# Gates and ups of a GEGLU block as pairs of 64-row half tiles

## The chip, the cores and the metric

The kernel runs on one core of a Trainium2 chip. The metric is the time of one execution on the device, in microseconds (us). A time is the median of several executions. Beside it stands one profiled execution of the same program, with its own time, its span (from the first instruction to the last) and a record of each instruction. PE is TensorE, DVE is VectorE, ACT is ScalarE, POOL is GpSimd and SP is SyncE, which here only starts DMA transfers. PEld stands for the weight loads of PE.

## The reference

One transformer layer on 2048 tokens of 448 features, in bfloat16. Attention and feed-forward block read the same normalised input and are added to the residual.

```python
xn = layernorm(x)                                     # x: [1, 2048, 448]
qkv = xn @ wqkv                                       # 16 heads of 28
scores = (q @ k^T) * 28**-0.5, kept where 0 <= i - j < 256
attn = (softmax(scores) @ v) @ wo
ffn = (gelu_tanh(xn @ w_gate) * (xn @ w_up)) @ w_down # 448 -> 1792 -> 448
out = x + attn + ffn
```

The gate and up products are the part that the change touches. Both contract over 448 features, which is three times 128 and a rest of 64. Each has 1792 output features, or 14 tiles of 128.

## The kernel before, in words

The 2048 tokens are worked through in four blocks of 512 (`qb` 0 to 3). The normalised input is held transposed in `xnT`, with features on the partitions. It has four chunks. Chunks 0 to 2 hold 128 features each. Chunk 3 holds the last 64 features twice, on the partitions 0 to 63 and again on 64 to 127.

**Order of the work.** Each block has an attention stage (`attention`) and then a gated stage (`gated`). In the attention stage PE computes scores (L612), ACT takes their exponentials (L618), and PE multiplies them with the values (`pv`, L572). Between the steps PE is fed with other work from generators in `Feed` objects. `share` and `drain` take from them by budgets written out by hand (`plan`, `PROJ`, `DOWN`, `UP1`). In block 0 this other work is the block's own q and k projections, some of its up products ("early" ups, `gen_up`, tile `ue`) and the projections of block 1. In blocks 1 and 2 it is the down projection of the block before (`gen_down`, tile `po`, L371 and L376) and the next block's projections. In block 3 it is a down projection and early ups. After the last gated stage the last down projection runs alone.

**Gates and ups.** An output tile needs three matmuls with 128 rows of features (`three`, which calls `mm3`, L228) and one with 64 rows (`half`, which calls `mm_half`, L234). The 64-row matmuls are issued in twos: one on the lower 64 rows of the PE array and one on the upper 64 rows. They share the array, and each writes its own PSUM bank. The weights of the last 64 features are therefore kept in `wgu3` and `wug3`, which hold gate and up rows on opposite halves of the partitions. Work goes in pairs of neighbouring output tiles, `f` and `f + 1`. `gated` collects the 64-row matmuls of two or three pairs into one stretch: the groups are (0, 2), (4, 8, 6), (10, 12) in blocks 0 and 3, and (0), (2, 4), (6, 8), (10, 12) in blocks 1 and 2. For the first pair of blocks 1 to 3 the 64-row matmuls are cut to 32 columns, the tile form that the `pv` matmuls behind them have. ACT applies the gelu (L460), and DVE multiplies with the up product (L467). An early up is copied from PSUM into `hT` by a DVE cast (L411), and is multiplied there later.

**PSUM banks.** There are eight banks. In the gated stage the gates use two tiles of two banks each (tag `s`). The ups, early ups, projections, `pv` and the down projection share two banks of tag `m` and one each of tags `d` and `o`. In the attention stage the scores take the four banks of `s`. In blocks 1 to 3 the early ups and projections then have the two `m` banks, which `pv` also uses for its two halves. There ACT copies one half (L556) and DVE adds the other to it (L557).

**Loads.** SP starts nearly all transfers in one order, and its transfers run in that order. Ahead of the first attention stage these are: x, the projection weights, `wu` with the up rows of `wug3` and `wgu3`, x of tokens 1024 to 1535, and a small piece of k weights (`w3k`). Behind them come four transposes of the normalised input of block 1 (L215), then x of the last tokens, gate weights, `wo` and `wd`.

A second path (`general_path`, entered when the plain softmax could overflow) isn't entered in the runs shown.

Of the kernel before, what the change touches and what calls it, by code (L numbers as in the profile page):

```python
# [16 lines left out]
P = 128  # L17
# [58 lines left out]
def kernel(  # L76
# [45 lines left out]
    def rows(w, c0, n):  # L122
        return w[c0 * P:(c0 + n) * P, :].rearrange("(c p) n -> p c n", p=P)

# [55 lines left out]
    xnT = const.tile([P, 4, S], bf16, name="xnT")  # L180
    qT = const.tile([P, 4, S], bf16, name="qT")
# [171 lines left out]
    UP1 = 1660  # L353
# [36 lines left out]
    def half(ps, f, gate, hi, ts, start, stop, m=P):  # L390

        w3 = wgu3 if gate != bool(hi) else wug3
        mm_half(ps, w3[:, f * P:(f + 1) * P], xnT[:, 3, ts], hi, start, stop, m)

    def three(ps, f, gate, ts, start, stop):
        w = wg if gate else wu
        mm3(ps, lambda c: w[:, c, f * P:(f + 1) * P], lambda c: xnT[:, c, ts], start, stop)

    def gen_up(qb, fs):

        ts = slice(qb * QB, (qb + 1) * QB)
        for f in fs:
            us = []
# [6 lines left out]
            for i in range(2):  # L410
                nc.vector.tensor_copy(out=hTs[qb][:, f + i, :], in_=us[i][:, :])  # L411
            yield -360

    def gated(qb, early, last_v, flush, hook):

        ts = slice(qb * QB, (qb + 1) * QB)
        hT = hTs[qb]
        turn = ["o" if down_tag[0] == "d" else "d", down_tag[0]] * 4

        def single(name, tag):  # L420
            return psum.tile([P, QB], f32, name=name, tag=tag, bufs=2 if tag == "m" else 1)[:, :]

        def begin(f, apart=False):
            last_tag[0] = turn[0] if f not in early else last_tag[0]
            pr = dict(f=f, us=[])
            if apart:
                pr["gs"] = [single("g0", tag) for tag in ("m", turn.pop(0))]
                return pr
            pr["gt"] = phase[0].pool.tile([P, 2, QB], f32, name="gt", tag="s")
            pr["gs"] = [pr["gt"][:, i, :] for i in range(2)]  # L430
            if f not in early:
                tags = ("m", turn.pop(0))
                if qb == 0 and f == 0:
                    tags = [ring[0][(ring[1] + i) % 3] for i in range(2)]
                    if "d" in tags:
                        turn.insert(0, "o")
                pr["us"] = [single("u0", tag) for tag in tags]
            return pr

        def dense(pr, start):  # L440
            f = pr["f"]
            gs = [(g, f + i, True) for i, g in enumerate(pr["gs"])]
            us = [(u, f + i, False) for i, u in enumerate(pr["us"])]
            for ps, fi, gate in (gs + us if f else us + gs):
                three(ps, fi, gate, ts, start, not start)

        def halves(pr, start, m):
            f = pr["f"]
            for i in range(2):
                if pr["us"]:  # L450
                    half(pr["gs"][i], f + i, True, 0, ts, start, not start, m)
                    half(pr["us"][i], f + i, False, 1, ts, start, not start, m)
                else:
                    half(pr["gs"][i], f + i, True, i, ts, start, not start, m)

        def end(pr):
            f = pr["f"]
            ge = work.tile([P, 2, QB], bf16, name="ge", bufs=2)
            if "gt" in pr:
                nc.scalar.activation(out=ge[:, :, :], in_=pr["gt"][:, :, :], func=ACT.Gelu_apprx_tanh)  # L460
            else:
                for i, g in enumerate(pr["gs"]):
                    nc.scalar.activation(out=ge[:, i, :], in_=g, func=ACT.Gelu_apprx_tanh)
            if not pr["us"]:
                nc.vector.tensor_tensor(out=hT[:, f:f + 2, :], in0=ge[:, :, :], in1=hT[:, f:f + 2, :], op=ALU.mult)
            for i, u in enumerate(pr["us"]):
                nc.vector.tensor_tensor(out=hT[:, f + i, :], in0=ge[:, i, :], in1=u, op=ALU.mult)  # L467
                flush()
            hook(f)

        for fs in ((0, 2), (4, 8, 6), (10, 12)) if qb in (0, 3) else ((0,), (2, 4), (6, 8), (10, 12)):
            prs = [begin(fs[0])]
            dense(prs[0], True)
            prs += [begin(f, len(fs) == 3 and f == fs[1]) for f in fs[1:]]
            for pr in prs:
                halves(pr, pr is not prs[0], 32 if qb and not fs[0] else P)
            if not fs[0]:
                last_v()
            end(prs[0])
            for pr in prs[1:]:  # L480
                dense(pr, False)
                end(pr)
# [49 lines left out]
    def attention(qb, feeds, aux, plan):  # L532
# [52 lines left out]
        if qb:  # L585
            feeds[0].run()
        steps = list(steps_of(qb))
        pvs = {4: 0, 6: 1, 9: 2} if qb else {4: 0, 7: 1, 10: 2}
        for i, (scores, ncol, edges) in enumerate(steps):
# [38 lines left out]
            if left == 1:  # L628
                drain(feeds)
            elif not qb:  # L630
                share(feeds + [Feed()], 1e12, 0)
            else:
                to = plan.get(i, 0)
                whole = sum(f.left for f in feeds) + STEP * left + PV * sum(j > i for j in pvs)
                ahead = STEP + PV * (i + 1 in pvs) + (360 if to > 1000 else 0)
                late = 400 if i == 0 else 0
                want = (whole - late) / (left + 0.2) + late - ahead - to
                if i in pvs:
                    had = feeds[0].left
                    share(feeds[:1], min(1100, want), 0)  # L640
                    want -= had - feeds[0].left
                share(feeds, want, to)
# [57 lines left out]
    transp(3, 1, nc.vector.tensor_copy, "d")  # L700
    pvs.append(alone("pv", "o"))
# [50 lines left out]

    for qb in range(NB):
# [11 lines left out]
        if qb == 0:  # L765
            new_hT(0)
            early = (2, 4, 8)
            feeds = [Feed((gen_qk(0, (1, 2, 3), [(t, pvs[t]) for t in (2, 3)]), 3 * QK1 + 360),
                          (gen_up(0, (2, 8)), 2 * UP1), (gen_proj(1), PROJ), (gen_up(0, (4,)), UP1))]
        else:  # L770
# [63 lines left out]
    with tc.If(n_ok < 1, preferred_fallthrough_block=True, label="general"):  # L834
        general_path(tc, locals_=dict(x_sb=x_sb, xnT=xnT, qT=qT, kT=kT, v_sb=v_sb, wg=wg, wu=wu, wgu3=wgu3, wd=wd, wo=wo,
                                      ident=ident, outv=outv))


def general_path(tc, locals_):
# [4 lines left out]
    with ExitStack() as st:  # L844
# [11 lines left out]
        for qb in range(NB):  # L856
            ts = slice(qb * QB, (qb + 1) * QB)
            for f in range(NF):
                fs = slice(f * P, (f + 1) * P)
                pg = ps.tile([P, QB], f32, name="pg", tag="pg")  # L860
                pu = ps.tile([P, QB], f32, name="pu", tag="pu")
                for i, (dst, w) in enumerate(((pg, L["wg"]), (pu, L["wu"]))):
                    for c in range(3):
                        nc.tensor.matmul(dst[:, :], lhsT=w[:, c, fs], rhs=xnT[:, c, ts], start=(c == 0), stop=False)
                    p0 = 64 * i
                    nc.tensor.matmul(dst[:, :], lhsT=L["wgu3"][p0:p0 + 64, fs], rhs=xnT[p0:p0 + 64, 3, ts], start=False, stop=True,
                                     tile_position=(p0, 0))
# [78 lines left out]
```

## Time and profile before

| | |
|---|---|
| median of 3 executions | 221.18 us (221.12 to 221.22) |
| the profiled execution's own time | 221.11 us |
| its span | 219.4 us |
| mean granted TensorE clock | 0.998 |
| PE busy | 213.0 us, 97% of the span, 2281 matmuls |
| DVE busy | 152.3 us, 69% |
| ACT busy | 133.3 us, 61% |
| POOL busy | 48.8 us, 22% |
| share of PE in the chain that ended last | 93% |

The profiled execution's own time is 1.7 us above its span. What the span says of a change can so be added to 221.11 us, which stands 0.07 us below the median. A matmul record is longer than the distance to the next one, because matmuls overlap at their ends. So the starts of matmuls tell more of PE's pace than their durations do.

### The profile page before, as it was taken

How to read it: one execution, taken by the hardware profiler on the slowest of the kernel's cores; microseconds unless marked ns; L12 is line 12 of the kernel's file. 1: busy time of each engine (PE TensorE's matmuls, PEld its weight loads, DVE VectorE, ACT ScalarE, POOL GpSimd, SP SyncE). 2: the span in 40 equal slices, each digit the busy share in tenths (PEclk: the TensorE clock that was granted, in tenths of full speed). 3: DMA queues.
4: the chain of work that ended last, by engine and by line, in shares of the span. 5: the costliest groups of instructions: out<-in, count | busy, mean ns of one | idle time of the engine just before them, and what ended most of it. 6: DMA issues, size and time to landing. Idle time of an engine off the chain costs nothing.

```text
span 219.4 us, 5439 instructions
## 1 busy us (share of the span) xinstructions
PE 213.0 (97%) x2281; PEld 95.6 (44%) x2281; DVE 152.3 (69%) x345; ACT 133.3 (61%) x131; POOL 48.8 (22%) x83
## 2 busy tenths in 40 slices
PE   6999999999999999999999999999999999999993
PEld 2433333444444454444444445444344445444562
DVE  5987896799666883679565795386356799479521
ACT  3588788662878875432878888233486777565000
POOL 5767987320000120022000022021000022022001
PEclk9999999999999999999999999999999999999999
DMA  6994799203100001102400000200000000000001
GB/s 191 300 302 80 180 318 308 51 1 75 45 0 24 24 24 27 20 1 44 75 1 24 23 1 24 52 14 0 0 3 21 25 3 24 24 1 0 22 28 44
DMA packets 18045, 13.30 MB, mean 61 GB/s; under 512 B 8704, under 2 KB 16992, under 8 KB 18016
## 3 DMA queue, kind: packets, MB, share of 16 engines
q1 hardware_dynamic: 17072, 12.62, 21.5%
q8 instruction: 19, 0.31, 0.6%
q10 hardware_dynamic: 944, 0.29, 0.5%
q14 instruction: 10, 0.08, 0.1%
HBM read 9.15 MB, written 2.18 MB: 52 GB/s over the span
## 4 chain that ended last, share of the span: by engine, by line
PE 93%; DVE 3%; DMA 1%; ACT 1%; issue 1%; DVEq 0%
PE po L376 20%; PE gt L228 16%; PE u L228 12%; PE sc L612 6%; PE po L371 6%; PE gt L234 5%; PE ue L228 5%; PE ov L572 5%; PE pq L228 4%; PE pv L228 4%; PE pk L228 3%; PE pq L234 1%; PE g L228 1%; DMA x_sb<-in_A_x_dram 1%; PE ue L234 1%; PE pv L234 1%
## 5 line engine op out<-in xcount | busy, mean ns | idle before, releaser
L618 ACT ACTIVATE p_sb<-sc 128x2048 bf16<-128x2048 f32 (+2 forms) x42 | 73.8, 1758 | 12.6 <-PE sc L612 8.2
L376 PE MATMUL po<-wd,hT 128*128 128x448 bf16 (+1 forms) x238 | 49.8, 342 | 0.0
L460 ACT ACTIVATE ge<-gt 128x1024 bf16<-128x1024 f32 x26 | 26.6, 1024 | 34.9 <-PE u L234 20.1
L538 POOL TENSOR_TENSOR oN<-oc,l 128x512 bf16<-128x512 f32 x12 | 16.0, 1332 | 137.8 <-DVE l L552 87.4
L228 PE MATMUL gt<-xnT,wg 128*128 128x512 bf16 x156 | 37.5, 380 | 0.0
L467 DVE TENSOR_TENSOR hT<-ge,u 128x512 bf16<-128x512 bf16 x40 | 25.7, 682 | 12.9 <-ACT ge L460 12.9
L376 PEld LDWEIGHTS <-hT 128*128 128x128 bf16 x238 | 21.5, 98 | 18.8 <-issue 2.6
L228 PE MATMUL u<-xnT,wu 128*128 128x512 bf16 x120 | 29.2, 379 | 0.0
L519 DVE TENSOR_TENSOR p_sb<-p_sb,masks 128x256 bf16<-128x256 bf16 (+1 forms) x90 | 26.8, 352 | 0.4 <-ACT p_sb L618 0.4
L228 PEld LDWEIGHTS <-wg 128*128 128x128 bf16 x168 | 15.3, 98 | 21.3 <-issue 4.5
L228 PEld LDWEIGHTS <-wu 128*128 128x128 bf16 x168 | 16.0, 98 | 19.2 <-issue 1.0
L557 DVE TENSOR_TENSOR oc<-oc,ov 128x512 f32<-128x512 f32 x12 | 8.2, 687 | 16.5 <-ACT oc L556 16.5
L612 PE MATMUL sc<-qT,kT 28*64 28x320 bf16 (+7 forms) x640 | 16.9, 263 | 0.2
L411 DVE CAST hT<-ue 128x512 bf16<-128x512 f32 x16 | 10.2, 682 | 8.3 <-PE ue L234 8.3
L371 PE MATMUL po<-wo,oN 128*128 128x448 bf16 (+1 forms) x68 | 15.9, 342 | 0.0
L381 DVE TENSOR_TENSOR res<-po,x_sb 128x448 bf16<-128x448 f32 (+1 forms) x17 | 10.0, 586 | 8.6 <-PE po L376 8.4
L529 POOL TENSOR_SCALAR_AFFINE_SELECT p_sb<-p_sb 128x512 bf16<-128x512 bf16 (+1 forms) x20 | 14.2, 730 | 5.5 <-ACT p_sb L618 5.4
L234 PE MATMUL gt<-xnT,wgu 64*128 64x512 bf16 (+1 forms) x67 | 12.7, 380 | 0.0
L556 ACT COPY oc<-ov 128x512 f32<-128x512 f32 x12 | 7.0, 584 | 8.7 <-PE ov L572 8.7
L228 PE MATMUL pq<-xnT,wqp 128*128 128x512 bf16 x45 | 12.2, 380 | 0.0
L544 DVE STREAM_TRANSPOSE l<-oc 128x512 f32<-128x512 f32 x16 | 11.3, 704 | 1.4 <-POOL oN L538 1.2
L228 PE MATMUL ue<-xnT,wu 128*128 128x512 bf16 x48 | 12.0, 380 | 0.0
(94 smaller groups left out, 242.7 us busy)
## 6 DMA issues: line engine op xcount, KB each, us to landing
out_dram<-res SPq DMA_DIRECT2D x15, 112.0 KB
x_sb<-in_A_x_dram SPq DMA_DIRECT2D x3, 448.0 KB
wu<-in_B_w_up_dram SPq DMA_DIRECT2D x1, 1344.0 KB
wg<-in_B_w_gate_dram SPq DMA_DIRECT2D x1, 1344.0 KB
wd<-in_B_w_down_dram SPq DMA_DIRECT2D x3, 448.0 KB
wraw<-in_A_wqkv_dram SPq DMA_DIRECT2D x2, 252.0 KB
wo<-in_A_wo_dram SPq DMA_DIRECT2D x4, 98.0 KB
wv<-in_A_wqkv_dram SPq DMA_DIRECT2D x1, 336.0 KB
```

The source lines that it names most:

```text
L228: nc.tensor.matmul(ps, lhsT=lhs(c), rhs=rhs(c), start=start and c == 0, stop=stop and c == 2, skip_group_check=True)
L234: nc.tensor.matmul(ps[c:c + m], lhsT=lhs[p0:p0 + 64, c:c + m], rhs=rhs[p0:p0 + 64], start=start, stop=stop, tile_position=(p0, c), skip_gr ...
L371: nc.tensor.matmul(po[:, 0:w], lhsT=oN[:, g, cs], rhs=wo[:, g, lo:up], start=(g == 0), stop=False, skip_group_check=True)
L376: nc.tensor.matmul(po[:, 0:w], lhsT=hT[:, f, cs], rhs=wd[:, f, lo:up], start=False, stop=(f == NF - 1), skip_group_check=True)
L460: nc.scalar.activation(out=ge[:, :, :], in_=pr["gt"][:, :, :], func=ACT.Gelu_apprx_tanh)
L467: nc.vector.tensor_tensor(out=hT[:, f + i, :], in0=ge[:, i, :], in1=u, op=ALU.mult)
L519: nc.vector.tensor_tensor(out=reg, in0=reg, in1=m, op=ALU.mult)
L529: nc.gpsimd.affine_select(out=reg, in_=reg, pattern=mid + [[1 if diag else -1, min(w, P)]], compare_op=ALU.is_ge, fill=0.0, base=0 if diag ...
L538: nc.gpsimd.tensor_tensor(out=oN[:, g, :], in0=oc[:, :], in1=inv, op=ALU.mult)
L544: nc.vector.transpose(out=l1[:, :, :].rearrange("p a b -> p (a b)"), in_=oc[:, :])
L612: nc.tensor.matmul(ss[k0:k0 + nk, j, col:col + nq], lhsT=kT[r, g, kt * P + k0:kt * P + k0 + nk], rhs=qT[r, g, qb * QB + q0:qb * QB + q0 + ...
L618: nc.scalar.activation(out=p_sb[:, :, 0:ncol], in_=ss[:, :, 0:ncol], func=ACT.Exp, scale=SCALE)
```

## The change

All gate and up products go as pairs of 64-row half tiles over seven chunks of 64 features. In a pair (`chunk`) the lower 64 rows of the array work on output tile `p` and the upper 64 rows on output tile `p + 7`, with the same chunk of features. Each output tile gets seven 64-row matmuls in place of three with 128 rows and one with 64. The weights are laid out for that: `wg` and `wu` hold, on partitions 0 to 63, all seven chunks of the first 896 output features, and on 64 to 127 those of the other 896. Each is loaded by two DMAs to 64 partitions. `wgu3` and `wug3` go.

Each chunk of features must stand on both halves of the partitions. `xnT` holds chunks 0 to 5 on one half only. So a second copy `xsw` of the first three tiles of `xnT`, for one block, is made with its halves swapped, by two DMAs on SP (`swap`). For block 0 it is started ahead of the first attention stage, and for the other blocks at the start of their own.

The gated stage has the fixed order up(0), gate(0), gate(1), gate(2) and so on, without groups. Early pairs become 1, 2, 4 in block 0 and 1, 2, 3, 4 in block 3 (four in place of five). In blocks 1 to 3 the attention stage no longer starts with a piece of the down projection. In block 3 the down projection takes the main budget, and the ups only the second one.

```diff
-    wg = const.tile([P, 3, F], bf16, name="wg")
-    wu = const.tile([P, 3, F], bf16, name="wu")
-    wgu3 = const.tile([P, F], bf16, name="wgu3")
-    wug3 = const.tile([P, F], bf16, name="wug3")
+    wg = const.tile([P, 7, F // 2], bf16, name="wg")
+    wu = const.tile([P, 7, F // 2], bf16, name="wu")
...
+    def load_ffn(dst, w):
+        wv64 = w.rearrange("(c p) n -> p c n", p=64)
+        for hi in range(2):
+            nc.sync.dma_start(out=dst[64 * hi:64 * hi + 64, :, :], in_=wv64[:, :, hi * (F // 2):(hi + 1) * (F // 2)])
...
-    nc.sync.dma_start(out=wu[:, :, :], in_=rows(B_w_up, 0, 3))
-    nc.sync.dma_start(out=wug3[0:64, :], in_=B_w_up[384:448, :])
-    nc.sync.dma_start(out=wgu3[64:128, :], in_=B_w_up[384:448, :])
+    load_ffn(wu, B_w_up)
...
+    xsw = const.tile([P, 3, QB], bf16, name="xsw")
...
+    def swap(qb):
+        ts = slice(qb * QB, (qb + 1) * QB)
+        for hi in range(2):
+            nc.sync.dma_start(out=xsw[64 * hi:64 * hi + 64, :, :], in_=xnT[64 - 64 * hi:P - 64 * hi, 0:3, ts])
+
+    def chunk(pair, w, p, qb, c):
+        for hi, ps in enumerate(pair):
+            r = slice(64 * hi, 64 * hi + 64)
+            ts = slice(qb * QB, (qb + 1) * QB)
+            x = xnT[r, 3, ts] if c == 6 else xnT[r, c // 2, ts] if c % 2 == hi else xsw[r, c // 2, :]
+            nc.tensor.matmul(ps, lhsT=w[r, c, p * P:(p + 1) * P], rhs=x, start=c == 0, stop=c == 6,
+                             tile_position=(64 * hi, 0), skip_group_check=True)
...
+    def gen_up(qb, ps):
+        for p in ps:
+            us = [bank("ue")[:, :] for _ in range(2)]
+            for c in range(7):
+                chunk(us, wu, p, qb, c)
+                if c == 2:
+                    yield 640
+                if c == 5:
+                    yield 640, HOLD
             for i in range(2):
-                us.append(bank("ue"))
-                three(us[i][:, :], f + i, False, ts, True, False)
-                yield (650, HOLD) if i else 650
-            for i in range(2):
-                half(us[i][:, :], f + i, False, i, ts, False, True)
...
+                nc.vector.tensor_copy(out=hTs[qb][:, p + 7 * i, :], in_=us[i])
+            yield -320
...
+        up(0)
+        gate(0)
+        end(0)
+        gate(1)
+        if 1 in early:
+            end(1)
+            gate(2)
+            up(2)
+        else:
+            gate(2)
+            up(1)
+            end(1)
+            up(2)
+        end(2)
+        for p in range(3, 7):
+            gate(p)
+            up(p)
+            end(p)
...
-        if qb:
-            feeds[0].run()
...
+                if qb == NB - 1:
+                    share(feeds[:1], want, 0)
+                    share(feeds, 0, to)
+                else:
+                    share(feeds, want, to)
...
     transp(3, 1, nc.vector.tensor_copy, "d")
+    swap(0)
...
-        nc.sync.dma_start(out=wgu3[0:64, :], in_=B_w_gate[384:448, :])
-        nc.sync.dma_start(out=wug3[64:128, :], in_=B_w_gate[384:448, :])
-        nc.sync.dma_start(out=wg[:, :, :], in_=rows(B_w_gate, 0, 3))
+        load_ffn(wg, B_w_gate)
...
-            early = (2, 4, 8)
+            early = (1, 2, 4)
...
-                early = (2, 4, 6, 8, 10)
+                early = (1, 2, 3, 4)
                 feeds.append(Feed((gen_up(3, early), UP1 * len(early))))
-                plan = {0: 1300, 2: 1300, 4: 1300, 6: 1300, 7: 1300}
+                plan = {2: 1280, 4: 1280, 6: 1280, 7: 1280}
+        if qb:
+            swap(qb)
         score_pool(1)
```

In `gated`, `up(p)` issues the seven pairs of both up tiles unless the pair is early, `gate(p)` those of both gate tiles and the gelu behind them, and `end(p)` the multiplications. `gate(0)` also holds the `pv` of the last head group, between its matmuls and its gelu.

More of the change, by code (lines that the diff above doesn't have):

```diff
@@ L352 @@
     DOWN = 4 * 3400
-    UP1 = 1660
+    UP1 = 1600
     STEP, PV = 450, 870
@@ L417, in gated @@
         hT = hTs[qb]
         turn = ["o" if down_tag[0] == "d" else "d", down_tag[0]] * 4
[L420 to L460, printed above, removed]
-            else:
[L462 to L482, printed above, removed]
+        us, ges = {}, {}
@@ new lines, in up @@
+        def up(p):
+            if p in early:
+                return
+            last_tag[0] = turn[0]
+            tags = ("m", turn.pop(0))
+            if qb == 0 and p == 0:
+                tags = [ring[0][(ring[1] + i) % 3] for i in range(2)]
+                if "d" in tags:
+                    turn.insert(0, "o")
+            us[p] = [psum.tile([P, QB], f32, name="u0", tag=tag, bufs=2 if tag == "m" else 1)[:, :] for tag in tags]
+            for c in range(7):
+                chunk(us[p], wu, p, qb, c)
@@ new lines, in gate, with end @@
+        def gate(p):
+            gt = phase[0].pool.tile([P, 2, QB], f32, name="gt", tag="s")
+            for c in range(7):
+                chunk([gt[:, i, :] for i in range(2)], wg, p, qb, c)
+            if not p:
+                last_v()
+            ges[p] = work.tile([P, 2, QB], bf16, name="ge", bufs=2)
+            nc.scalar.activation(out=ges[p][:, :, :], in_=gt[:, :, :], func=ACT.Gelu_apprx_tanh)
+        def end(p):
+            ge = ges.pop(p)
+            if p in early:
+                nc.vector.tensor_tensor(out=both(hT, p), in0=ge[:, :, :], in1=both(hT, p), op=ALU.mult)
+            else:
+                for i, u in enumerate(us.pop(p)):
+                    nc.vector.tensor_tensor(out=hT[:, p + 7 * i, :], in0=ge[:, i, :], in1=u, op=ALU.mult)
+                    flush()
+            hook(2 * p)
@@ L857, in general_path @@
             ts = slice(qb * QB, (qb + 1) * QB)
+            for hi in range(2):
+                nc.sync.dma_start(out=L["xsw"][64 * hi:64 * hi + 64, :, :], in_=xnT[64 - 64 * hi:P - 64 * hi, 0:3, ts])
             for f in range(NF):
-                fs = slice(f * P, (f + 1) * P)
+                hi, p = divmod(f, 7)
+                r = slice(64 * hi, 64 * hi + 64)
                 pg = ps.tile([P, QB], f32, name="pg", tag="pg")
                 pu = ps.tile([P, QB], f32, name="pu", tag="pu")
[L862 to L867, printed above, removed]
+                for dst, w in ((pg, L["wg"]), (pu, L["wu"])):
+                    for c in range(7):
+                        x = xnT[r, 3, ts] if c == 6 else xnT[r, c // 2, ts] if c % 2 == hi else L["xsw"][r, c // 2, :]
+                        nc.tensor.matmul(dst[:, :], lhsT=w[r, c, p * P:(p + 1) * P], rhs=x, start=(c == 0), stop=(c == 6),
+                                         tile_position=(64 * hi, 0))
                 ge = wk.tile([P, QB], bf16, name="gge")
```

20 lines of the change are left out of this document (4 added, 16 removed).

## The prediction, made before the changed kernel was run

> **What bounds the kernel now.** I read the page first: busy shares, and the chain that ended last. Then the waits of PE.
>
> ```profile
> PE 213.0 (97%) x2281; PEld 95.6 (44%) x2281; DVE 152.3 (69%) x345; ACT 133.3 (61%) x131; POOL 48.8 (22%) x83
> ...
> PE 93%; DVE 3%; DMA 1%; ACT 1%; issue 1%; DVEq 0%
> ...
> PE wps L190 <- DVE wo L167: 2.0, 1, 2.0
> PE tp L223 <- DVE xn L209: 0.3, 1, 0.3
> ```
>
> PE is busy from end to end, and both waits that are listed fall before 8 us. So whatever shortens PE's own stream shortens the kernel, and any new wait of PE lengthens it by its full size. To price the stream I read PE's timeline where a gated stage of block 2 goes from 128-row matmuls to 64-row pairs and back, with its weight loads. The first column is the start; of each pair only the first matmul is shown.
>
> ```profile
> 146.16 1.46 PE L228 MATMUL gt<-xnT,wg 128*128 128x512 bf16 x6
> 147.45 1.46 PE L228 MATMUL u<-xnT,wu 128*128 128x512 bf16 x6
> 148.84 0.39 PE L234 MATMUL gt<-xnT,wgu 64*128 64x512 bf16 x1
> ...
> 149.07 0.38 PE L234 MATMUL gt<-xnT,wgu 64*128 64x512 bf16 x1
> ...
> 149.28 0.38 PE L234 MATMUL gt<-xnT,wgu 64*128 64x512 bf16 x1
> ...
> 149.50 0.38 PE L234 MATMUL gt<-xnT,wgu 64*128 64x512 bf16 x1
> ...
> 149.81 0.39 PE L228 MATMUL gt<-xnT,wg 128*128 128x512 bf16 x1
> ...
> 148.84 0.55 PEld L234 LDWEIGHTS <-wgu 64*128 64x128 bf16 x8 [0.42 <-issue]
> ```
>
> Six 128-row matmuls take 147.45 - 146.16 = 1.29 us, or 0.215 each. A pair of 64-row matmuls takes the same 0.215 (149.07, 149.28, 149.50). The eight weight loads of the stretch are over at 149.39, before the last pair starts, so they run beside earlier pairs. A change of tile form costs 0.31 - 0.215 = 0.095 us (149.50 to 149.81), and the first one behind it 0.01 more (148.84 to 149.07). Taken from the starts of all matmuls in this trace, the other kinds of change cost 0.09 to 0.11 as well.
>
> The new copy and the new weight layout are DMAs to 64 partitions, so I read the DMA engines by stretches (last two columns: share of time busy, GB/s).
>
> ```profile
> 9.50:13.00 3.50, 3.50 (x25) 1.19 (x24) 2.98 (x9) 1.41 (x4) 3.01 (x13) 1.00 0.98 369
> 13.50:15.50 2.00, 1.84 (x14) 0.66 (x12) 1.85 (x6) 2.00 (x3) 0.44 (x2) 1.00 1.01 217
> 29.50:31.50 2.00, 2.00 (x14) 0.70 (x12) 1.71 (x4) 1.81 (x3) 1.87 (x4) 1.00 1.01 401
> ```
>
> The first and third are the 128-partition loads of `wu` and `wg`. The second is mostly the 64-partition loads of `wug3` and `wgu3`: engines as busy, but 217 GB/s.
>
> **Part 1: PE's stream, -2.1 us.** A pair of output tiles cost six 128-row slots and one slot of halves. It now costs seven slots of pairs, all of 0.215: no difference. The changes of form I counted in the order of the instructions as built: 153 before, 133 after. The gated stages go from 8, 8, 8 and 6 to 3 each, the attention stages of blocks 0 and 3 from 39 to 37 and 28 to 27, and the last down projection from 0 to 1. 20 x 0.105 = 2.1 us. Bounds: 20 x 0.09 = 1.8 and 20 x 0.11 = 2.2.
>
> **Part 2: the copy for block 0 comes late, +1.2 us.** The first early up starts at 19.55 and its second matmul needs `xsw`. SP starts that copy early (it waits only for the fourth tile of `xnT`, some 10 us), but its data run behind what SP started before. `wu`'s data began at 9.1 us (its first 3,584-byte packet). Now all of it, 1.606 MB, goes to 64 partitions at 217 GB/s: 7.4 us, to 16.5. Then x of tokens 1024 to 1535, 0.459 MB: between 13.15 and 17.6 that and the two small weight loads moved 0.918 MB, or 206 GB/s, so some 2.0 us, to 18.5. `w3k` takes 0.1, and the copy, 0.393 MB at 217, 1.8: 20.4. The x load's last packet started at 17.6 and landed at 18.05, so 0.5 more: 20.9, against a need at 19.65. That is 1.2 us of standing PE, with everything queued behind it in PE's order. Bounds: if x and the copy run at 369, 9.1 + 7.4 + 1.2 + 0.1 + 1.1 + 0.5 = 19.4, so 0; with all 2.49 MB at 206, 9.1 + 12.1 + 0.5 = 21.7, so 2.0. I take the middle, because `wu` itself is the case that the 217 row shows. [...]
>
> **Part 3: a pair needs both of its banks at once, +1.9 us.** Until now the first tile's three matmuls (0.65 us) covered the emptying of the second bank. Two places lose that cover.
>
> Entry of the gated stage of block 0. The banks of u are those of the last early up, emptied by casts (37.70, two in 1.29 us). From the end of the early up to a free first bank: 0.17 us end of a matmul (record 0.38 against spacing 0.215), 0.04 to the cast, 0.68 cast, 0.05 back: 0.94. Scores (0.2) and a change (0.1) lie between: 0.6 us stay open. Bounds 0.3 and 0.65.
>
> Attention of block 3. `pv` holds both `m` banks.
>
> ```profile
> 171.35 0.69 DVE L557 TENSOR_TENSOR oc<-oc,ov 128x512 f32<-128x512 f32 x1 [1.31 <-ACT oc L556]
> 171.71 1.03 PE L228 MATMUL ue<-xnT,wu 128*128 128x512 bf16 x4
> ...
> 176.93 0.69 DVE L557 TENSOR_TENSOR oc<-oc,ov 128x512 f32<-128x512 f32 x1 [0.47 <-ACT oc L556]
> 177.19 1.03 PE L228 MATMUL ue<-xnT,wu 128*128 128x512 bf16 x4
> ...
> 179.01 1.29 DVE L411 CAST hT<-ue 128x512 bf16<-128x512 f32 x2
> 179.75 1.46 PE L228 MATMUL ue<-xnT,wu 128*128 128x512 bf16 x6
> ```
>
> The second bank comes free at 172.04, 177.62 and 180.30, with 0.05 for the signal 0.4, 0.5 and 0.6 us behind these three starts. At the last the kernel already waits 0.1. So 0.4 + 0.5 + 0.5 = 1.4, less some 0.1 for places that shift: 1.3. Bounds: 0.4 if the moved down projection spreads the ups, and 4 x 0.65 = 2.6 if all four meet a full bank.
>
> **Part 4: gate(2) waits for gelu(0), +0.4 us.** In blocks 1 and 2 the old order put 2.6 us of gates and ups between the `pv` and the next use of the first gate tile. Now only gate(1) lies there, 7 x 0.215 = 1.5.
>
> ```profile
> 139.89 1.47 PE L228 MATMUL gt<-xnT,wg 128*128 128x512 bf16 x6
> 140.13 0.58 ACT L556 COPY oc<-ov 128x512 f32<-128x512 f32 x1 [3.18 <-PE ov L572]
> 140.61 1.03 ACT L460 ACTIVATE ge<-gt 128x1024 bf16<-128x1024 f32 x1
> ```
>
> ACT copies the `pv` first; the gelu ends at 141.64, plus 0.05. gate(2) is ready at 139.89 + 1.5 = 141.4: some 0.2, twice. Bounds 0.1 and 0.6.
>
> **What I cost at nothing.** The other three copies: issued at the end of the gated stage before; the nearest first use is some 7 us later (block 3), against some 3 us for a copy with its fixed part. Without that cover up to 3 us each. Gate weights: 1.606 MB at 217 from 26.5 is 34, needed at 39; `wo` and `wd`, some 2 us later, are needed from 56. On SP the transposes of block 1 run behind the copy, so the first lands near 22 in place of 18.7; its tile is needed at 24.2, and from there PE is late itself. Of the last pair, `hT` tile 6 is now the 11th matmul of the down projection, not the 13th: needed 10 x 0.19 = 1.9 us behind the last up, made by about 0.9. The early multiplications read with a stride; even at 1.36 us for 0.65 they stay under a gate's 1.5.
>
> **Sum.** -2.1 + 1.2 + 0.6 + 1.3 + 0.4 = +1.4. From the profiled execution's 221.11 (0.07 below the median of the runs): **222.5 us**.
>
> **Rivals.** (a) The waits are hidden: copy in time at the fast rate, banks free. What speaks for it is the queue's fast rows, and that later ups meet emptier banks; against it, every cover above is shorter than its wait. -2.1 + 0.0 + 0.3 + 0.4 + 0.1 = -1.3: 219.8 us, faster. The copy decides: with the waits of parts 3 and 4 at these lower ends, the kernel stays below its old time while the copy's wait is under 1.3 us. (b) A near tie: copy in time, bank waits as priced: -2.1 + 2.3 = +0.2, 221.3. (c) The copy meets the worst rates and the bank waits their upper ends: -2.1 + 2.0 + 0.65 + 2.6 + 0.6 = +3.75, some 224.9. (d) The pairs don't hold 0.215 over long stretches; the trace shows at most four in a row. If each of the 392 costs what the first behind a change costs, +0.01 x 392 = 3.9 more: 226.4. [...]
>
> **How the numbers follow.** Forecast 0.55; (a) 0.13; (b) 0.17; (c) 0.09; (d) 0.05; (e) 0.01. Times of this kernel spread by 0.1 us, so about 0.2% (0.44 us) can be told from no change. Faster is (a), 0.13; same is (b), 0.17; slower is the rest, 0.70. The range drops half of (a) and most of (c), and all of (d) and (e): 220.5 to 224.3.
>
> **What would show it.** Changes of form in PE's stream down to 133 with pairs still 0.215 apart; the first `ue` of block 0 standing near 20.9 for the copy; a gap of 0.6 before block 0's first `u`; gaps of 0.3 to 0.6 before `ue` in block 3; 0.2 before the third gate of blocks 1 and 2. A copy landed before 19.6, or pairs further apart than 0.22, would make the forecast wrong.

## The result, and the profile after

The changed kernel takes 225.35 us (median of 6 executions, 223.51 to 226.54), beside 221.20 us for the kernel before on the same chip (6 executions, 220.92 to 221.62). The ratio is 1.0173, with an interval of 1.0148 to 1.0199. It is slower, as forecast, but above the range that was given. The profiled execution took 223.96 us (span 222.1, mean granted clock 0.999), so it is one of the quick ones of its kernel. An execution more than 1.5% above the fastest of its kernel is left out of the ratios below; there is one, of 227.70 us.

The page of the changed kernel, busy shares and the chain that ended last:

```profile
PE 213.2 (96%) x2575; PEld 99.5 (45%) x2575; DVE 149.1 (67%) x344; ACT 132.9 (60%) x129; POOL 49.0 (22%) x83
...
PE 86%; DMA 7%; SPq 2%; ACT 2%; issue 1%; DVE 1%; ACTq 0%; DVEq 0%
```

PE is busy as long as before (213.2 us against 213.0), but the span is 2.7 us longer, and a DMA now stands in the chain with 7% instead of 1%. The list of PE's waits names it:

```profile
PE ue L409 <- DMA xsw<-xnT: 2.2, 1, 2.2
PE wps L195 <- DVE wo L171: 2.0, 1, 2.0
PE u L409 <- DVE hT L427: 0.2, 1, 0.2
```

In the kernel before, the first early up of block 0 ran through, six matmuls in 1.47 us:

```profile
19.55 1.47 PE L228 MATMUL ue<-xnT,wu 128*128 128x512 bf16 x6
```

In PE's timeline of the changed kernel (first column: start; second: length of the records in us) the two matmuls of a pair start together when nothing holds them (both at 88.56 us at the head of the gated stage of block 1). Where the first starts alone, the distance to the next line is a standing of PE.

```profile
19.33 0.39 PE L409 MATMUL ue<-xnT,wu 64*128 64x512 bf16 x1
21.93 0.39 PE L409 MATMUL ue<-xsw,wu 64*128 64x512 bf16 x2 [2.21 <-DMA xsw<-xnT]
22.14 0.39 PE L409 MATMUL ue<-xnT,wu 64*128 64x512 bf16 x2
22.36 0.39 PE L409 MATMUL ue<-xsw,wu 64*128 64x512 bf16 x2
...
39.97 0.39 PE L409 MATMUL u<-xnT,wu 64*128 64x512 bf16 x1
40.59 0.39 PE L409 MATMUL u<-xsw,wu 64*128 64x512 bf16 x2 [0.24 <-DVE hT L427]
...
91.93 1.09 PE L409 MATMUL gt<-xnT,wg 64*128 64x512 bf16 x4
92.65 0.58 PE L409 MATMUL gt<-xsw,wg 64*128 64x512 bf16 x2
...
172.19 0.39 PE L409 MATMUL ue<-xnT,wu 64*128 64x512 bf16 x1
172.71 0.39 PE L409 MATMUL ue<-xsw,wu 64*128 64x512 bf16 x2
...
178.18 0.39 PE L409 MATMUL ue<-xnT,wu 64*128 64x512 bf16 x1
178.56 0.39 PE L409 MATMUL ue<-xsw,wu 64*128 64x512 bf16 x2
...
181.00 0.39 PE L409 MATMUL ue<-xnT,wu 64*128 64x512 bf16 x1
181.41 0.39 PE L409 MATMUL ue<-xsw,wu 64*128 64x512 bf16 x2
```

Behind a standing the pairs follow each other every 0.215 us (21.93, 22.14, 22.36). The standings are 2.60 us for the copy (19.33 to 21.93), 0.62 at the first up of block 0, and 0.52, 0.38 and 0.41 at early ups of block 3, where a standing of 0.15 us before scores at 171.34 comes on top. The line at 91.93 holds four matmuls, of which the next pair should follow 0.43 us later; it comes after 0.72, so the third gate stands for 0.29 us, and as long again in block 2.

So the profiled execution adds up: -2.1 (changes of form) + 2.6 + 0.6 + 1.4 (block 3: 1.46 less the 0.1 that stood before) + 0.6 = +3.1, less some 0.2 by which PE came earlier to the first early up (19.33 against 19.55): +2.9. Its time is 223.96 - 221.11 = 2.85 us longer. The median of the six executions stands another 1.4 us higher, and this profile does not show why.

### The profile page after: what moved, and what is told of

It is laid out like the page before. It is cut to its first block, busy times and chain, and to the rows that moved or that the text cites. A ratio compares the mean times of both kernels' runs of the same rounds, so it can differ in the third digit from the quotient of the medians.

```text
span 222.1 us, 6044 instructions
## 1 busy us (share of the span) xinstructions
PE 213.2 (96%) x2575; PEld 99.5 (45%) x2575; DVE 149.1 (67%) x344; ACT 132.9 (60%) x129; POOL 49.0 (22%) x83
## 4 chain that ended last, share of the span: by engine, by line
PE 86%; DMA 7%; SPq 2%; ACT 2%; issue 1%; DVE 1%; ACTq 0%; DVEq 0%
PE po L381 20%; PE gt L409 18%; PE u L409 14%; PE po L376 6%; PE ue L409 5%; PE sc L613 5%; DMA xsw<-xnT 5%; PE ov L575 5%; PE pq L233 4%; PE pv L233 3%; PE pk L233 3%; DMA wraw<-in_A_wqkv_dram 2%; PE pq L239 1%; ACT ge L456 1%; PE pv L239 1%
## 5 line engine op out<-in xcount | busy, mean ns | idle before, releaser
L456 ACT ACTIVATE ge<-gt 128x1024 bf16<-128x1024 f32 x28 | 28.6, 1024 | 35.5 <-PE gt L409 34.9
L409 PE MATMUL gt<-xnT,wg 64*128 64x512 bf16 x224 | 46.0, 376 | 0.2
L409 PE MATMUL gt<-xsw,wg 64*128 64x512 bf16 x168 | 40.3, 376 | 0.0
L464 DVE TENSOR_TENSOR hT<-ge,u 128x512 bf16<-128x512 bf16 x42 | 26.9, 680 | 14.2 <-PE u L409 11.0
L409 PE MATMUL u<-xnT,wu 64*128 64x512 bf16 x168 | 35.1, 376 | 0.0
L409 PEld LDWEIGHTS <-wu 64*128 64x128 bf16 x392 | 20.3, 94 | 26.5 <-issue 7.5
L409 PE MATMUL u<-xsw,wu 64*128 64x512 bf16 x126 | 30.1, 376 | 0.2 <-DVE hT L427 0.2
L409 PEld LDWEIGHTS <-wg 64*128 64x128 bf16 x392 | 20.0, 94 | 22.2 <-issue 1.1
L427 DVE CAST hT<-ue 128x512 bf16<-128x512 f32 x14 | 9.0, 686 | 8.6 <-PE ue L409 8.6
L613 PEld LDWEIGHTS <-kT 28*64 28x64 bf16 (+1 forms) x640 | 7.8, 102 | 11.4 <-issue 9.8
```

The lines of the kernel that those rows point to most:

```text
L409: nc.tensor.matmul(ps, lhsT=w[r, c, p * P:(p + 1) * P], rhs=x, start=c == 0, stop=c == 6, tile_position=(64 * hi, 0), skip_group_check=True)
L456: nc.scalar.activation(out=ges[p][:, :, :], in_=gt[:, :, :], func=ACT.Gelu_apprx_tanh)
L464: nc.vector.tensor_tensor(out=hT[:, p + 7 * i, :], in0=ge[:, i, :], in1=u, op=ALU.mult)
L613: nc.tensor.matmul(ss[k0:k0 + nk, j, col:col + nq], lhsT=kT[r, g, kt * P + k0:kt * P + k0 + nk], rhs=qT[r, g, qb * QB + q0:qb * QB + q0 + ...
```

## The experiments

**Theory:** the loss is the copy of block 0, which lands behind everything that SP started ahead of it; in executions where PE stands longer for it the granted clock falls as well, and that makes the times above 225. **Rivals:** the copy itself lands at very different times, with no part for the clock; or the pairs cost something of their own in all blocks.

**The changed kernel once more, for a second profile.**

> The changed kernel once more, to see an execution of the slower kind (its times lie from 223.5 to 226.5 us; the profiled one, 223.96 us, has a granted clock of 0.999, the executions above 225 us one near 0.992). Theory A (clock): the copy lands at nearly the same time in all executions, some 2.6 us late, and in some of them this standing of PE is enough for the granted clock to fall for some microseconds behind it; an execution near 225.5 would show matmuls 0.43 us apart in place of 0.215 for about 3 to 4 us behind the copy, worth 1.5 to 2 us. Rival B (the copy itself varies): an execution near 225.5 shows the copy landing some 1.5 to 2 us later than 21.9, with matmuls behind it 0.215 apart.

Four executions took 223.76, 224.53, 226.16 and 227.70 us, beside 221.49 for the kernel before. The ratio, 1.0155 (1.0104 to 1.0207), is that of the first three. The longest one is the profiled one, so it is read here only for what else happened in it. PE's timeline, then the waits of PE:

```profile
23.31 0.61 PE L409 MATMUL ue<-xsw,wu 64*128 64x512 bf16 x2 [3.26 <-DMA xsw<-xnT]
23.69 0.65 PE L409 MATMUL ue<-xnT,wu 64*128 64x512 bf16 x2
24.12 0.65 PE L409 MATMUL ue<-xsw,wu 64*128 64x512 bf16 x2
24.54 0.65 PE L409 MATMUL ue<-xnT,wu 64*128 64x512 bf16 x2
```

```profile
PE ue L409 <- DMA xsw<-xnT: 3.3, 1, 3.3
```

Both happened. The copy came 1.4 us later than in the other profile, and behind it the pairs are 0.43 us apart, twice 0.215: the granted clock is 0.50 from 21.80 to 28.63 us. So neither the theory nor the first rival is the whole of it. A shorter execution shows the same fall further down, in the profile of the run with the gelu ahead of the `pv` copy.

**PE kept busy through the wait.** Ten matmuls whose result is thrown away are put ahead of the first early up of block 0.

```diff
             us = [bank("ue")[:, :] for _ in range(2)]
+            for _ in range(10 if qb == 0 and p == 1 else 0):
+                nc.tensor.matmul(us[0], lhsT=xnT[:, 0, 0:P], rhs=xnT[:, 0, 0:QB], start=True, stop=True, skip_group_check=True)
```

> Ten matmuls of 512 columns whose result is thrown away (10 x 0.215 = 2.15 us) stand ahead of the first early up of block 0, in the time in which PE waits for the copy. The result is the reference's. Theory A (the clock falls because PE stands): all executions at 223.8 to 224.3 us with a granted clock of 0.998 or more; the wait for the copy shrinks from 2.6 to 0.4 us and no time is gained beside the profiled execution of the change, but the spread up to 226.5 goes. Rival B (the copy's landing varies): the times still spread from 223.5 to 226.5.

224.21 us (223.50 to 224.87, 4 executions), with mean clocks of 0.997 to 1.0. The ten matmuls take 2.2 us at 0.215, about what PE would have stood. The times above 225 are gone, as is the half clock, in these four executions. A spread of 1.4 us stays, where 0.5 (223.8 to 224.3) was expected, and the kernel before spread by 0.7 on this chip. That the rest of it is the copy's is likely, but not shown by this run.

**The copy ahead of x.** The load of x of tokens 1024 to 1535 goes behind the copy on SP.

```diff
     load_ffn(wu, B_w_up)
-    nc.sync.dma_start(out=x_sb[:, 8:12, :], in_=xv[:, 8:12, :])
...
     swap(0)
+    nc.sync.dma_start(out=x_sb[:, 8:12, :], in_=xv[:, 8:12, :])
```

> The load of x for tokens 1024 to 1535 moves behind the copy for block 0 in SP's order; nothing else changes. Theory (the copy is late because its data stand in SP's queue behind wu and this load): 0.459 MB at some 210 GB/s is 2.2 us, so the copy lands near 19.7 in place of 21.9, the wait falls from 2.6 to some 0.4 us, and the time to 221.8 us (223.96 - 2.2), with a granted clock of 0.998 in all executions. Rival (the copy between the halves is slow by itself, whatever stands ahead of it): a wait of over 1.5 us stays, and 223 us or more.

222.75 us (222.20 to 223.56, 5 executions; ratio 1.0072, 1.0047 to 1.0097). The copy's last packet ends at 19.18 us, not 21.00, and the waits of PE have

```profile
PE ue L408 <- DMA xsw<-xnT: 0.4, 1, 0.4
```

where the changed kernel has 2.2. One line moved on one queue brings the ratio from 1.0155 to 1.0072 on this chip, about 1.8 of 3.4 us. In the two profiles PE stands 0.78 us in place of 2.60, which is 1.8 less. It did not reach the 221.8 that was expected, because the wait did not go entirely.

**No copy.** All copies are left out, and the pairs read `xnT` where they read `xsw`. Part of the products is then computed from the wrong features.

```diff
-        for hi in range(2):
-            nc.sync.dma_start(out=xsw[64 * hi:64 * hi + 64, :, :], in_=xnT[64 - 64 * hi:P - 64 * hi, 0:3, ts])
+        return
...
-            x = xnT[r, 3, ts] if c == 6 else xnT[r, c // 2, ts] if c % 2 == hi else xsw[r, c // 2, :]
+            x = xnT[r, 3, ts] if c == 6 else xnT[r, c // 2, ts]
```

> All eight copies are left out, and the pairs read xnT in place of xsw; so half of the products of six of the seven chunks take the wrong features, and the output is not the reference's. PE's stream is the same. It gives the rest of the sum: fewer changes of form -2.1, waits for banks and gelu of +2.4 as the trace of the change has them (0.62 + 0.15 + 0.52 + 0.38 + 0.41 + 0.28 + 0.28 = 2.64, less 0.1 to 0.2 that the kernel before has at the same places). Theory: 223.96 - 2.59 = 221.4 us. Rival (a part of the loss is hidden in something else, such as pairs that run slower than single matmuls): 222 us or more. Second rival (the waits move when the copy is gone and are absorbed): 220.5 us or less.

221.79 us (221.44 to 222.12, 10 executions), 0.3 us above the 221.49 of the kernel before; ratio 1.0013 (1.0002 to 1.0023). That is 0.4 above the 221.4 that was expected, and under the 222 of the rival. So the rest of the change is worth +0.3 us, and no sign is left of a cost of the pairs themselves.

**The copy in time, with its data.** `wu` is loaded in two parts. Columns 0 to 639 of each half, which the early pairs 1, 2 and 4 need, stay where the whole load was. The rest and x go behind the copy.

```diff
-    def load_ffn(dst, w):
+    def load_ffn(dst, w, a=0, b=F // 2):
...
-    load_ffn(wu, B_w_up)
-    nc.sync.dma_start(out=x_sb[:, 8:12, :], in_=xv[:, 8:12, :])
+    load_ffn(wu, B_w_up, 0, 5 * P)
...
     swap(0)
+    nc.sync.dma_start(out=x_sb[:, 8:12, :], in_=xv[:, 8:12, :])
+    load_ffn(wu, B_w_up, 5 * P, 7 * P)
```

> The changed kernel with only the order of the start loads mended: columns 0 to 639 of each half of wu ahead of the copy, columns 640 to 895 and x of tokens 1024 to 1535 behind it; the gelu and the down projection of block 3 as in the changed kernel. Theory (the copy's wait is the whole excess over the part of the sum without it): the copy lands near 18.5, a microsecond ahead of its use, PE does not stand there in any execution, the clock stays at full, and the time is that of the changed kernel without copies, 221.8 us, with a spread as small as that one's (0.7 us). Rival (the copy costs time in other ways too, by what its data and its later uses in blocks 1 to 3 delay): 222.3 us or more.

221.58 us (221.36 to 222.73, 12 executions), beside 221.48 before; ratio 1.0013 (1.0000 to 1.0025). All mean clocks are 0.996 or more. Eleven of the twelve lie within 0.7 us, as expected; the one of 222.73 us, at full clock, stays unexplained. The first part of `wu` ends at 16.00 us and the copy at 17.68. The copy is no longer among the waits of PE:

```profile
PE wps L194 <- DVE wo L170: 2.0, 1, 2.0
PE tp L227 <- DVE xn L213: 0.8, 2, 0.6
PE u L408 <- DVE hT L426: 0.2, 1, 0.2
```

That is the time without copies (221.79) within what can be told. The rival, that the copies cost time in other places too, falls, and the loss of the change, but for 0.1 to 0.3 us, is shown to be the place of one copy in the queue.

**Both banks at once, in the kernel before.** No part of the change but this: the early ups, and the first up pair of block 0, interleave the matmuls of their two tiles.

```diff
-            us = []
-            for i in range(2):
-                us.append(bank("ue"))
-                three(us[i][:, :], f + i, False, ts, True, False)
-                yield (650, HOLD) if i else 650
+            us = [bank("ue") for i in range(2)]
+            for c in range(3):
+                for i in range(2):
+                    nc.tensor.matmul(us[i][:, :], lhsT=wu[:, c, (f + i) * P:(f + i + 1) * P], rhs=xnT[:, c, ts], start=c == 0,
+                                     stop=False, skip_group_check=True)
+                    if 2 * c + i == 2:
+                        yield 650
+            yield 650, HOLD
...
+            if qb == 0 and not f:
+                for c in range(3):
+                    for ps, fi, gate in us:
+                        nc.tensor.matmul(ps, lhsT=wu[:, c, fi * P:(fi + 1) * P], rhs=xnT[:, c, ts], start=c == 0, stop=False,
+                                         skip_group_check=True)
+                us = []
```

> The kernel before, with one part of the change alone: its early ups, and the first up pair of the gated stage of block 0, take both PSUM banks at once, the dense matmuls of the two tiles in turns in place of one tile after the other. No pairs of 64 rows, no copy, no new order of the work. Theory (a matmul group that takes both banks at once must wait for the second one): a standing of some 0.6 us ahead of the first up of block 0 and of 0.3 to 0.6 at three or four of the five early ups of block 3, together +1.0 to +1.9 us: about 222.6 us beside a kernel before at 221.3. Rival (these waits in the changed kernel come from its moved down projection and its fewer early pairs, not from needing both banks): no change, 221.2 to 221.5 us.

222.83 us (222.56 to 224.35, 6 executions) beside 221.41; ratio 1.0076 (1.0051 to 1.0101): +1.4 us, inside the theory's 1.0 to 1.9. Two of the places in PE's timeline:

```profile
37.70 0.39 PE L450 MATMUL u<-xnT,wu 128*128 128x512 bf16 x1
38.33 1.24 PE L450 MATMUL u<-xnT,wu 128*128 128x512 bf16 x5 [0.24 <-DVE hT L414]
...
180.45 0.38 PE L406 MATMUL ue<-xnT,wu 128*128 128x512 bf16 x1
181.04 1.24 PE L406 MATMUL ue<-xnT,wu 128*128 128x512 bf16 x5 [0.22 <-DVE hT L414]
```

Less the 0.215 of a matmul these stand for 0.42 and 0.38 us. Two more early ups of block 3 stand for 0.18 and 0.26: in all 1.24 of the 1.4. So taking two banks at once is enough for a cost of the size of part 3, without the new order of the work.

**The gelu ahead of the `pv` copy.** Added to the copy ahead of x:

```diff
-                if g == 2 or qb == NB - 1 and g == 3:
+                if g > 1:
                     behind.append((oc, ov))
```

> The changed kernel with the x load of tokens 1024 to 1535 behind the copy, and with the copy of the pv halves of head group 3 of blocks 1 and 2 put behind the gelu on ACT, not ahead of it. Theory (the third gate of blocks 1 and 2 waits for the gelu because ACT copies the pv first): both standings of 0.28 us go, and the time is 222.75 - 0.57 = 222.2 us. Rival (the copy only moves, and what waits for it stands as long): 222.75 us, or more if the add that needs the copy comes late.

222.39 us (221.48 to 224.53, 12 executions; ratio 1.0049, 1.0027 to 1.0072), near the 222.2 that was expected, but the copy is still late in it: PE stands 2.24 us for it in the profile. In its profile the third gate of block 1 follows after 0.44 us (93.07 to 93.51), where the changed kernel has 0.72. Its profiled execution (224.53 us, mean clock 0.992) shows the fall of the clock once more; it is read in the last section.

**All mends together.** This one with `wu` in two parts as above, and the down projection of block 3 at other steps.

```diff
-                plan = {2: 1280, 4: 1280, 6: 1280, 7: 1280}
+                plan = {1: 1280, 2: 1280, 4: 1280, 7: 1280}
```

> The kernel of the run before this one, with wu loaded in two parts (columns 0 to 639 of each half ahead of the copy, 640 to 895 behind it and behind the x load), and with the down projection of block 3 put at steps 1, 2, 4 and 7 in place of 2, 4, 6 and 7, so that less of its early ups meet a bank that pv just left. Theory (the copy's wait is a matter of the bytes ahead of it in SP's queue): wu's first part ends near 15.2 us, the copy lands near 17.5, two us ahead of its use, and no standing is left there, so the time stands where the changed kernel without copies stood less the two waits behind the gelu: 221.8 - 0.6 = 221.2, less some 0.4 if one of the waits in block 3 goes: 220.8 to 221.3 us, level with the kernel before or just under it. Rival (the copy is slow in itself, whatever is ahead of it): it lands near its use again, with a spread of 1 us between executions, 222 us and more.

221.01 us (220.61 to 221.42, 12 executions) beside 221.41 before: ratio 0.9979 (0.9968 to 0.9990). It beats both kernels, by a margin at the edge of what can be told. ACT's timeline of the changed kernel, then of this one, at the head of the gated stage of block 1:

```profile
91.08 0.59 ACT L559 COPY oc<-ov 128x512 f32<-128x512 f32 x1 [3.29 <-PE ov L575]
91.56 2.03 ACT L456 ACTIVATE ge<-gt 128x1024 bf16<-128x1024 f32 x2
```

```profile
88.46 1.02 ACT L455 ACTIVATE ge<-gt 128x1024 bf16<-128x1024 f32 x1 [2.54 <-PE gt L408]
89.38 0.58 ACT L558 COPY oc<-ov 128x512 f32<-128x512 f32 x1
```

With the gelu first the third gate follows without a standing, in PE's timeline of this kernel:

```profile
90.06 0.81 PE L408 MATMUL gt<-xnT,wg 64*128 64x512 bf16 x4
90.49 0.59 PE L408 MATMUL gt<-xsw,wg 64*128 64x512 bf16 x2
```

0.43 us against 0.72. Twice 0.29 is 0.58, and 221.58 - 221.01 is 0.57 (0.75 by the ratios; the two ran on different chips). So the gelu accounts for most or all of the difference to the kernel with only `wu` in two parts. The moved down projection was not run by itself. By the profile it gave at most some 0.2 us: the early ups in block 3 stand twice, for 0.60 and 0.67 us, 1.27 in all, in place of 0.15, 0.52, 0.38 and 0.41, or 1.46.

**Two queues for `wu`.** The upper half of `wu` starts on ACT's queue.

```diff
-            nc.sync.dma_start(out=dst[64 * hi:64 * hi + 64, :, :], in_=wv64[:, :, hi * (F // 2):(hi + 1) * (F // 2)])
+            (nc.scalar if hi and dst is wu else nc.sync).dma_start(out=dst[64 * hi:64 * hi + 64, :, :], in_=wv64[:, :, hi * (F // 2):(hi + 1) * (F // 2)])
```

> The changed kernel with the two halves of wu (one to the partitions 0 to 63, one to 64 to 127) started from two queues, so that both move at the same time. Theory (a transfer to 64 partitions is slow, 190 GB/s, because only half of the partitions take data): both halves together move at more than 300 GB/s where they overlap, wu is over by some 14 us, the copy lands before 19 us and its wait goes: near 221.8 us if the loads ahead of it aren't delayed. Rival (the 1,792-byte packets or the order of the source are slow, whichever partitions they go to): wu moves at 190 to 220 GB/s in all, the copy lands near 21 us as before, and the time is 224 us or more.

226.01 and 227.40 us, two executions: slower still, and no answer to its question. ACT's half moved from 5.4 to 10.5 us, ahead of loads that the start needs, and SP's half from 13.0 to 17.8, so they never ran side by side. PE stood at the start, and 3.41 us at half clock followed, 13.75 to 17.16 (last section). By the waits of PE:

```profile
PE tp L228 <- DVE xn L214: 3.6, 1, 3.6
```

**Short packets to all partitions.** The question put otherwise: the kernel before, with its 128-partition load of `wu` cut into two of 896 columns, so that the packets have 1,792 bytes as in the changed kernel.

```diff
-    nc.sync.dma_start(out=wu[:, :, :], in_=rows(B_w_up, 0, 3))
+    for a in (0, F // 2):
+        nc.sync.dma_start(out=wu[:, :, a:a + F // 2], in_=rows(B_w_up, 0, 3)[:, :, a:a + F // 2])
```

> The kernel before, with its load of wu (128 partitions, 3,584-byte packets, 369 GB/s) cut into two loads of 896 columns each, so that its packets are 1,792 bytes as in the changed kernel, but still go to all 128 partitions. Theory (the 190 to 217 GB/s are those of a transfer to 64 partitions): such packets take some 0.07 to 0.09 us in the mean, not 0.141, and move at 330 to 370 GB/s. Rival (the packet's size sets the rate): 0.14 us each, 200 GB/s. The time of the kernel stays, 221.2 us, by the first; by the second wu ends 3 us later, still ahead of its use at 20, and the time stays too.

The stretch from 9.5 to 13 us in which `wu` moves, first of this kernel, then of the changed one (last columns: granted clock, DMA share, GB/s):

```profile
9.50:13.00 3.50, 3.50 (x25) 1.19 (x24) 3.01 (x9) 1.51 (x5) 2.97 (x14) 1.00 1.03 352
```

```profile
9.50:13.00 3.50, 3.50 (x25) 1.18 (x24) 3.01 (x9) 1.51 (x5) 2.97 (x14) 1.00 1.07 222
```

Packets of the same size take 0.082 us in the mean to 128 partitions and 0.141 us to 64. So in these runs the 64 partitions set the rate, not the size of the packet. The time of the kernel is 221.83 us against 221.48 (8 executions; ratio 1.0014, 1.0002 to 1.0027), near its old time as expected.

## Why the prediction was wrong

**Part 1 (changes of form, -2.1) was right.** The trace has 133 changes, each 0.09 to 0.11 us where PE does not wait, and pairs stay 0.215 us apart in long runs: 77 from 92.64 to 109.04 us, 0.216 each, every one with new weights for the same rows. Rivals (d) and (e), which put a cost on each of the 392 pairs, are out.

**Part 2 (the copy late by 1.2) is the step that failed**, and in two ways.

First, the size. The mechanism was right: the copy waits its turn in SP's queue (started from 10.09 us on, first packet at 18.56). But its wait was 2.6 us, above the upper bound of 2.0. Against the forecast's chain the packets of the profiled execution went so:

| | forecast | measured |
|---|---|---|
| projection weights ahead of `wu` over | 9.1 | 9.96 |
| `wu` over | 16.5 | 17.65 |
| x over | 18.5 | 19.16 |
| copy's last packet over | 20.4 | 21.00 |
| second matmul of the pair could start | 20.9 | 21.93 |
| it was wanted | 19.65 | 19.33 |

The rate was not the error: the stretches show 222 and 219 GB/s in all, and `wu`'s packets alone 216 between 10.0 and 15.9 us, where 217 had been taken. The first packet of `wu` was taken as the start of its full rate, while 0.19 MB of the load ahead of it still moved beside it, until 9.96; at 217 GB/s that is 0.9 us that the sum left out. And from the copy's last packet to PE 0.93 us passed, not 0.5 (0.70 to 1.06 in the other three profiles in which PE waited for it). The 0.5 was the landing of another load, without the start of PE behind it.

Second, what the forecast did not see at all. The time at which the copy lands is not one number. It moves with the loads ahead of it in the queue:

| us | projection weights over | `wu` (its first part) over | copy over | PE stands |
|---|---|---|---|---|
| the changed kernel | 9.96 | 17.65 | 21.00 | 2.60 |
| the same, second profile | 11.18 | 19.22 | 22.61 | 3.65 |
| copy ahead of x | 9.95 | 17.33 | 19.18 | 0.78 |
| the same, gelu first | 10.91 | 18.56 | 20.53 | 2.24 |
| `wu` in two parts | 10.08 | (16.00) | 17.68 | 0.27 |
| all mends | 11.56 | (16.65) | 18.41 | 0.27 |

The rows stand in twos with the same start loads, and in each two the later projection weights go with the later copy, by 0.7 to 1.6 us. The kernel before has no use of a load near there, and its times spread by 0.7 us (6 executions) to 1.1 us (23). That is more than the 0.1 that the prediction had from three. And the granted clock fell to half with the standings of 3.65 us (for 6.83 us) and 2.24 us (for 3.41 us), though not with that of 2.60. A mean clock of 0.992 fits one fall of 3.41 us (half of that is 1.7, of some 218 us: 0.008), and four of the six executions of the result have 0.991 or 0.992. They took 225.14 to 226.54 us; the two at 0.998 and 0.999 took 223.51 and 223.96. The four stand 2.1 us above the two in the mean: 1.7 for the half clock, and some 0.4 left for a longer standing. Spread over six executions, four falls of 1.7 are 1.1 of the 1.4 us by which the median stands above the profile. That is an estimate, and keeping PE busy agrees with it: no fall, and 224.21 us.

**Part 3 (two banks at once, +1.9) was right**: 0.62 for 0.6, and 1.36 for 1.3. The kernel before with this part alone lost 1.4 us. One place was missed: the first early up of block 0 stands some 0.27 us even when the copy is early (last two rows of the table). By the times it waits for its second bank: it goes on 0.06 and 0.04 us behind the end of ACT's cast of q (L285: 19.48 and 20.01 us). In the changed kernel the copy hides it.

**Part 4 (gate waits for gelu, +0.4) was right in its mechanism and somewhat short**: 0.29 us twice. Putting the gelu first removed it.

**The items at nothing** left no trace: behind 20 us PE's timeline of the changed kernel has no standing above 0.1 us but those named. The copy for block 3 takes 3.0 us from its start on SP to its last packet (160.48 to 163.47), and the early multiplications 0.65 us in the median (one of seven 1.70; in the kernel before one of eight 1.80). With the copy in time the kernel takes 221.58 us, where the sum without part 2 gives 221.3: the near tie of rival (b) is what the rest of this change is worth.

The median stands 2.85 us above the forecast: 1.4 us from the size of one wait, and 1.4 us, by the estimate above, from the executions in which the wait was longer still and the clock fell behind it, which had no term. Of the four executions without a fall (223.51, 223.76, 223.96 and 224.53 us) three lie inside the range that was given; all those with a fall lie above it. That the new sizes of parts 3 and 4 did not move the sum was partly luck: 0.3 us more, against 0.2 by which the first early up started earlier.

## What to carry to other kernels

A transfer that is needed a few microseconds after a long queue of others is not one term with a middle value: add up what is ahead of it, the tail of the load before included, and if it lands near its use, move it ahead of bytes that aren't needed yet (here the order of the start loads was worth some 3.5 us, a ratio of 1.0173 against one of 1.0013). A standing of PE is also to be priced with the clock that may fall with it: here it fell with standings of 2.24 and 3.65 us and not with one of 2.60, and 3.41 us at half clock are 1.7 us lost, by the estimate above. And where matmuls are paired over two banks, the emptying of the second bank loses the cover that the first tile's matmuls gave (here 0.62 us at one place and 1.36 at others).

## What the runs showed of the hardware

**Half clock with a standing of PE.** The granted clock was 0.50 for 3.41 us with the gelu first (21.99 to 25.40 us) and with two queues (13.75 to 17.16), and for 6.83 us in the second profile of the changed kernel (21.80 to 28.63). The columns are a stretch, its length, PE's busy time, then the other engines, and behind them the granted clock. The first rows are of the kernel with the copy ahead of x and the gelu first, then the one with two queues: 3.41 us ahead of the half clock, and the half clock. The last rows are of the changed kernel in its first profile, 3.41 us with the end of the standing, and 4 us of what followed:

```profile
18.58:21.99 3.41, 1.49 (x16) 0.63 (x17) 1.42 (x3) 2.76 (x3) 2.41 (x5) 1.00 1.36 225
21.99:25.40 3.41, 3.41 (x30) 1.11 (x27) 1.29 (x2) 0.00 (x0) 2.53 (x11) 0.50 1.37 145
```

```profile
10.34:13.75 3.41, 1.36 (x9) 0.73 (x10) 1.74 (x5) 0.00 (x0) 2.73 (x12) 1.00 1.09 272
13.75:17.16 3.41, 3.41 (x11) 0.87 (x10) 1.81 (x7) 1.40 (x4) 0.00 (x0) 0.50 1.05 220
```

```profile
20.30:23.71 3.41, 1.78 (x21) 0.87 (x25) 0.28 (x1) 1.03 (x1) 2.79 (x8) 1.00 1.54 130
...
23.00:27.00 4.00, 4.00 (x47) 1.59 (x44) 2.77 (x5) 2.03 (x2) 2.44 (x12) 1.00 0.96 230
```

PE was busy for 1.49 and 1.36 us of the 3.41 us ahead of the half clock, and for 1.59 us of those ahead of it in the second profile of the changed kernel (18.39 to 21.80). There the first 3.42 us at half clock had PE busy for 1.91 us, and 3.41 us more at half clock followed. In the first profile of the changed kernel the clock stayed at 1.00, though PE stood for longer (2.60 us) than with the gelu first (2.24). So the length of a standing alone did not decide it, and what does stays open.

**A load to 64 partitions** moved at 222 GB/s and packets of the same size to 128 at 352, with the DMA engines equally busy (1.07 and 1.03).

What made the start loads end a microsecond later in some executions than in others was not looked into.
